# An attention and mixture-of-experts kernel: where memory rows are gated, when copies are issued, and which engine splits weights

## The chip, the cores and the metric

The kernel runs on one core of a Trainium2 chip. The metric is the device time of one execution in microseconds. The core has five instruction streams, each in program order: PE (TensorE, matrix products), ACT (ScalarE), DVE (VectorE), POOL (GpSimd) and SP, which here issues nearly all DMA transfers.

## The reference, cut to what matters

```
scores = (q @ k.T) / 8, causal;  local = softmax(scores) @ v
q_p = elu(q) + 1
mem = (q_p @ M_prev) / (q_p @ z_prev + 1e-6)
x = g * mem + (1 - g) * local          # g = sigmoid(beta), per head
h = relu(x @ w1[e]);  out += p[:, e] * (h @ w2[e])      # e = 0..3
```

There are 4 batches of 8 heads, 576 positions of 64 features each, so 2304 tokens of 512 features; four experts map 512 to 1024 to 512. All is float32 at the interface. The kernel gets its accuracy from split operands: a tensor is written as a high part (rounded) and a low part (the rest), and a product is three matmuls, high by high, high by low and low by high.

## The kernel before, in words

**Attention** is cut into runs (one batch and either its query blocks 0 and 1, called joint, or its blocks 2 to 4) and each run into four tasks, one for a pair of heads. The first run is written out by hand as a list of words (`ORDER`, in `first_run`). Tasks 0 to 27 are numbered over the other runs; tasks 0 to 11 are the joint ones. Each task is a set of steps, and each step stands in a list with a slot (its time on a planner's scale), a rank within the slot and a weight. The steps named below are `batch_load` (L234: loads z_prev broadcast to all partitions as `zb` and M_prev as `mr`, once per run; L239 multiplies `zb` by the gate on POOL), `t_phi1` to `t_phi4` (L300 to 343: elu, its product with `zb` in `rl`, its normaliser `rn`, the normalised `qp`), `t_trq` and `t_trk` (L381, L411: transpose q or k on PE and split it into `qa`, `qb` or `kha`, `khb`, `kl` by ACT and DVE) and `t_cpq` and `t_cpk` (L396, L420: DMA copies within the chip's memory, of q's high part to `qz` and of k's high parts to the other half of the partitions). The scores (`j_qk`, L474) read `qa`, `qz`, `kha`, `khb` and `kl`. `t_load` (L282) fetches q, k and v of a later task.

**Experts** run as phases. A phase is one half of one expert's hidden features for a group of 256 tokens or for two groups at once. Groups start at phases 0, 5, 8, 16 and 16 (`START`) and last 8 phases each, so that phases 0 to 4 and 13 to 15 hold a single group (`ALONE`) and the others two; after phase 23 (`PASS` is 24) eight more phases take the remaining tokens in another form. A phase has 16 parts of the first product (`mm1`, L862: four blocks `fc` of 128 hidden features, four parts each) and then the second product (`mm2`, L887: per tile of 128 tokens four parts, which read `w2s[0]` to `w2s[3]` in turn). After the last part of a block ACT writes the relu's high part `hh` (L880) and DVE its low part `hl` (L881).

**Weights** come by DMA into six buffers `stg`, a fixed order ahead (`w_dma`, L194). `w_prep` (L212) takes the next one: the high part by ACT (L225) or by POOL (L227), the low part always by POOL (L228), and then issues the next `w_dma` on SP, which waits until a buffer is free. A block of w1 for the next phase is prepared during the second product of the phase before; a block of w2 is prepared at the first part of the same block of the first product, by the call `after()` in `mm1`. In `first_run` the words w0 to w7 prepare w1 and w2 of phase 0, with high parts by POOL; between w1 and w2, between w3 and w4 and between w6 and w7 steps of the coming tasks are run, `batch_load` of task 0's run among them just ahead of w4.

**Interleaving**: a planner walks through the parts of the phases. Ahead of each part it runs steps while the weights done so far lie below a straight line against the estimated cost of the parts done. Before a group's first phase it runs all steps that the group's tokens need, and then `x_split` (L820) copies the group's tokens as a high part by ACT (L828) and a low part (L830) by DVE or POOL.

Of the kernel before, what the change touches and what calls it, by code (L numbers as in the profile page):

```python
# [11 lines left out]
ALU = mybir.AluOpType  # L12
# [37 lines left out]
def tile_attention_moe(  # L50
# [13 lines left out]
    nc = tc.nc  # L64
    P = 128
    B, H, S, D = q.shape
# [8 lines left out]
    CA, CB = (0, 1), (2, 3, 4)  # L75
# [23 lines left out]
    START = [0, 5, 8, 16, 16]  # L99
    PASS = START[-1] + NPH  # L100
# [13 lines left out]
    def ctile(shape, dt, name, pool=cst):  # L114
        return pool.tile(shape, dt, tag=name, name=name, bufs=1)

    def f(ap):
        return ap.bitcast(F32)
# [13 lines left out]
    gate = ctile([P, H], F32, "gate")  # L132
# [5 lines left out]
    for i in range(2):  # L138
# [49 lines left out]
    ALONE = [  # L188
        i for i in range(PASS) if sum(s_ <= i < s_ + NPH for s_ in START) == 1
    ]  # L190
# [3 lines left out]
    def w_dma():  # L194
        j = wpos["dma"]
        if j >= len(wseq):
            return
        wpos["dma"] += 1
        i, kind, fc = wseq[j]
        e, hf = halves[i]  # L200
        f0 = (hf * HF + fc) * P
        t = sp.tile([P, DM], F32, tag="stg", name=f"stg{j}", bufs=NSTG + 2)
        stg[j] = t
        if kind == "1":
            nc.sync.dma_start(
                out=t.rearrange("p (c f) -> p c f", c=NKD),
                in_=w1[e, :, f0 : f0 + P].rearrange("(c p) f -> p c f", p=P),
            )
        else:
            nc.sync.dma_start(out=t, in_=w2[e, f0 : f0 + P, :])  # L210

    def w_prep(i, kind, pool=False):  # L212
        act = (kind == "1" or i in ALONE or i >= PASS - 1) and not pool
        j = wpos["prep"]
        if j >= len(wseq) or wseq[j][0] != i or wseq[j][1] != kind:
            return
        wpos["prep"] += 1
        fc = wseq[j][2]
        t = stg.pop(j)
        hi, lo = (w1s if kind == "1" else w2s)[fc]  # L220
        if kind == "1":
            hi = hi.rearrange("p c f -> p (c f)")
            lo = lo.rearrange("p c f -> p (c f)")
        if act:
            nc.scalar.activation(hi, t, AF.Copy)  # L225
        else:
            nc.gpsimd.tensor_scalar(hi, t, 1.0, 1.0, ALU.mult, ALU.mult)  # L227
        nc.gpsimd.tensor_tensor(lo, t, f(hi), ALU.subtract)  # L228
        w_dma()


    bdat = {}

    def batch_load(r):  # L234
        b = r[0]
        zb = att.tile([P, H, D], F32, tag="zb", name=f"zb{b}_{r[1][0]}", bufs=2)
        nc.sync.dma_start(out=zb, in_=z_prev[b : b + 1].partition_broadcast(P)[:, 0])
        if b or r[1] == CB:
            nc.gpsimd.tensor_tensor(  # L239
                zb, zb, gate.unsqueeze(2).to_broadcast([P, H, D]), ALU.mult  # L240
            )
        mr = att.tile([P, H, D], F32, tag="mr", name=f"mr{b}_{r[1][0]}", bufs=1)
        for i in range(2):
            nc.sync.dma_start(
                out=mr[i * D : (i + 1) * D], in_=M_prev[b].rearrange("h d e -> d h e")
            )
        bdat[r] = [zb, mr, None]
# [16 lines left out]
    for b, cs in RUNS[1:]:  # L264
        for a in range(NPAIR):
            t = Task()
# [41 lines left out]
    def t_phi2(t):  # L308
        n = len(t.cs)
        t.qp = att.tile([P, 3, 2, D], F32, tag="qp", name=f"qp{t.i}", bufs=2)  # L310
        t.rl = att.tile([P, 3, 2, D + 1], F32, tag="rl", name=f"rl{t.i}", bufs=1)
        nc.vector.scalar_tensor_tensor(
            t.qp[:, 0:n], t.nat["q"][:, 0:n], 1.0, t.ex[:, 0:n], ALU.add, ALU.max
        )
        zb = bdat[t.run][0][:, 2 * t.a : 2 * t.a + 2].unsqueeze(1)
        nc.gpsimd.tensor_tensor(
            t.rl[:, 0:n, :, 0:D], t.qp[:, 0:n], zb.to_broadcast([P, n, 2, D]), ALU.mult
        )
        nc.gpsimd.tensor_scalar(
            t.rl[:, 0:n, :, D],  # L320
            gate[:, 2 * t.a : 2 * t.a + 2].unsqueeze(1).to_broadcast([P, n, 2]),
            1e-6,
            1.0,
            ALU.mult,
            ALU.mult,
        )
# [18 lines left out]
    def tr(dst, src, n):  # L345
        nc.tensor.transpose(dst, src, ident[0:n, 0:n])  # L346

    def to_tile(name):
        return ps.tile([P, 512], F32, tag="to", name=name, bufs=2)
# [28 lines left out]
    def flat(ap):  # L378
        return ap.rearrange("p j d -> p (j d)")

    def t_trq(t):  # L381
        pt = to_tile(f"tq{t.i}")
        qk, last = t.qk, t.nk == NCH
        w = len(t.cs) * P
        for i in range(len(t.cs)):

            tr(pt[:, i * P : (i + 1) * P], flat(t.nat["q"][:, i]), P)
        if last:
            tr(pt[:, w : w + P], flat(t.nat["k"][:, 4]), P)
        split_q(pt, qk["qa"], qk["qb"], w, SCALE)  # L390
        if last:
            split_k(pt[:, w:], qk, 4 * P, D)
        if t.i < 2:
            t_cpq(t)

    def t_cpq(t):  # L396
# [14 lines left out]
    def t_trk(t):  # L411
        pt = to_tile(f"tk{t.i}")
        m = min(t.nk, NCH - 1)
        for c in range(m):
            tr(pt[:, c * P : (c + 1) * P], flat(t.nat["k"][:, c]), P)
        split_k(pt, t.qk, 0, m * P)
        if t.i < 2:
            t_cpk(t)

    def t_cpk(t):  # L420
# [323 lines left out]
    for t in tasks:  # L744
        s0 = t.s0
        ld = -9 + t.i if t.i < 2 else s0 - 7
        PQ = PR
        n = len(t.cs)
        if t.run not in seen:
            seen.add(t.run)  # L750
            ev(s0 - (9 if t.i else 8), 9, lambda r=t.run: batch_load(r))
            ev(s0 + (2 if t.joint else 3), 9 if t.joint else 0.1, lambda r=t.run: batch_prep(r))
            if t.cs == CB and t.b == 0:
                for i in range(2):
                    ev(s0 - 12, 9, lambda i=i: zeros(i))
        ev(ld, 6.3 if t.cs == CA else 8, lambda t=t: t_load(t))
        ev(s0 + PQ["phi1"][0], PQ["phi1"][1], lambda t=t: t_phi1(t))
        ev(s0 + PQ["phi2"][0], PQ["phi2"][1], lambda t=t: t_phi2(t), 0.0, dv(n * P))
        ev(
            s0 + PQ["phi3"][0],  # L760
            PQ["phi3"][1],
            lambda t=t: t_phi3(t),
            0.0,
            600.0 if t.joint else 750.0,
        )
        ev(s0 - 3, 20, lambda t=t: t_phi4(t))
        ev(s0 + PQ["trq"][0], PQ["trq"][1], lambda t=t: t_trq(t), 109.0 * n, 2 * dv(n * P))
        ev(s0 + PQ["trk"][0], PQ["trk"][1], lambda t=t: t_trk(t), 109.0 * t.nk, 2 * dv(4 * P))
        if t.i >= 2:
            ev(s0 + PQ["trq"][0] + 1, 0.5, lambda t=t: t_cpq(t))  # L770
            ev(s0 + PQ["trk"][0], 2.4, lambda t=t: t_cpk(t))
        ev(s0, PQ["v"], lambda t=t: t_v(t))
        ev(
            s0 + PQ["trqp"][0 if t.joint else 2],
            PQ["trqp"][1],
            lambda t=t: t_trqp(t),
            109.0 * n,
            2 * dv(t.nq),
        )
    for i, s in slots.items():  # L780
        w = wid(s.c)
        t = s.t
# [37 lines left out]
    def x_split(n):  # L820
        for tt in range(2):
            o0 = (n % 2) * GW + tt * P
            o = slice(o0, o0 + P)
            r = rslot.pop((n, tt))
            rfree.append(r)
            rfree.sort()
            r = slice(r * P, (r + 1) * P)
            nc.scalar.activation(xh[:, :, o], xr[:, :, r], AF.Copy)  # L828
            sub = nc.gpsimd if n == 3 or (n == 4 and tt) else nc.vector
            sub.tensor_tensor(xl[:, :, o], xr[:, :, r], f(xh[:, :, o]), ALU.subtract)  # L830


# [29 lines left out]
    def mm1(i, fc, cols, after):  # L862
        wh, wl = w1s[fc]
        pt = []

        def part(c):
            if c == 0:
                pt.append(ps.tile([P, 512], F32, tag="moe", name=f"h{i}_{fc}", bufs=3))
                after()
            for z, (w_, x_) in enumerate(((wh, xh), (wh, xl), (wl, xh))):  # L870
                nc.tensor.matmul(  # L871
                    pt[0][:, cols],
                    lhsT=w_[:, c],
                    rhs=x_[:, c, cols],
                    start=(c == 0 and z == 0),
                    stop=(c == NKD - 1 and z == 2),
                )
            if c == NKD - 1:
                h_, l_ = hh[fc][:, cols], hl[fc][:, cols]
                nc.scalar.activation(h_, pt[0][:, cols], AF.Relu)  # L880
                nc.vector.scalar_tensor_tensor(  # L881
                    l_, pt[0][:, cols], 0.0, f(h_), ALU.max, ALU.subtract
                )

        return [lambda c=c: part(c) for c in range(NKD)]

# [721 lines left out]
```

## Time and profile before

| | us |
|---|---|
| runs of before: median (lowest, highest) | 1018.58 (1015.73, 1021.09) |
| the profiled execution | 1019.5 |
| its span, from the first to the last instruction | 1017.7 |
| PE busy in the span | 990.3 |
| ACT, DVE, POOL busy | 547.2, 650.4, 597.4 |
| mean granted clock of PE | 0.989 of full |

A busy PE is not a PE at its peak: its instructions overlap, and at half the clock the same product is busy for twice as long. So both the idle time of PE and the stretches of lowered clock are to be read.

### The profile page before, as it was taken

The page shows a single profiled execution, that of the slowest core. Times are in us where ns is not written, and L with a number is a line of the kernel's source. Part 1 is how long each engine was busy: PE and PEld are TensorE (multiplying, and loading weights), DVE is VectorE, ACT ScalarE, POOL GpSimd, SP SyncE. Part 2 cuts the span into 40 slices and gives each one's busy share as a digit, 9 for nine tenths or more (in the row PEclk, how much of TensorE's full clock was granted, in tenths as well). Part 3 has the DMA queues.
Part 4 walks back from the last instruction along what each step waited for, and adds up shares of the span by engine and source line. Part 5 has one row for each costly group of instructions (what it writes and reads, how often), then busy time and mean ns, then how long its engine had stood idle before and what let it go on. Part 6 is the DMA issues. An engine that isn't in the chain of part 4 may idle for free.

```text
span 1017.7 us, 16092 instructions
## 1 busy us (share of the span) xinstructions
PE 990.3 (97%) x5118; PEld 832.3 (82%) x5118; DVE 650.4 (64%) x1669; ACT 547.2 (54%) x1274; POOL 597.4 (59%) x614
## 2 busy tenths in 40 slices
PE   8798989999999999999999999999999999999998
PEld 6687878887888889888888888878888888888887
DVE  6477867887887878878777788664153342442533
ACT  7476745666666668866666665554243242342430
POOL 5578865775567547966564665394563554635630
PEclk9799989999999999999999999999999999999999
DMA  6566553544553446654453443222121121211102
GB/s 150 131 166 188 155 141 104 136 127 117 123 139 101 121 138 168 178 160 125 120 134 101 108 107 96 59 94 83 52 58 48 51 55 50 62 42 52 53 1 83
DMA packets 192149, 106.24 MB, mean 104 GB/s; under 512 B 99648, under 2 KB 170432, under 8 KB 192064
## 3 DMA queue, kind: packets, MB, share of 16 engines
q1 hardware_dynamic: 191760, 105.07, 38.6%
q8 instruction: 41, 0.67, 0.3%
q14 instruction: 44, 0.36, 0.1%
q10 hardware_dynamic: 304, 0.14, 0.1%
HBM read 90.09 MB, written 4.72 MB: 93 GB/s over the span
## 4 chain that ended last, share of the span: by engine, by line
PE 86%; POOL 4%; DMA 3%; DVE 2%; ACT 2%; issue 1%; SPq 1%; ACTq 0%; POOLq 0%; DVEq 0%
PE y L900 19%; PE h L871 18%; PE y L1172 17%; PE x L1096 9%; PE z L1096 4%; PE pt L346 4%; PE sp L612 4%; PE o L722 4%; PE y L1096 2%; POOL w2l L228 1%; PE tq L346 1%; PE sp L474 1%; PE tk L346 1%; PE o L560 1%; POOL w L228 1%
## 5 line engine op out<-in xcount | busy, mean ns | idle before, releaser
L228 POOL TENSOR_TENSOR w2l<-stg,w2h 128x512 fp32r<-128x512 f32 x128 | 167.7, 1314 | 146.2 <-ACT w2h L225 140.9
L871 PE MATMUL h<-xh,w 128*128 128x512 f32 (+1 forms) x768 | 248.5, 373 | 1.2 <-POOL w L228 1.2
L228 POOL TENSOR_TENSOR w<-stg,w 128x512 fp32r<-128x512 f32 x96 | 127.2, 1330 | 146.6 <-ACT w L225 135.6
L871 PEld LDWEIGHTS h<-xh,w 128*128 128x128 f32 x768 | 141.1, 192 | 18.8 <-POOL w L228 1.4
L900 PE MATMUL y<-w2h,hh 128*128 128x512 f32 x320 | 137.0, 428 | 2.0 <-POOL w2h L227 1.8
L871 PE MATMUL h<-xl,w 128*128 128x512 f32 (+1 forms) x384 | 137.6, 358 | 0.0
L900 PE MATMUL y<-w2l,hh 128*128 128x512 f32 x320 | 126.9, 397 | 3.0 <-POOL w2l L228 3.0
L900 PE MATMUL y<-w2h,hl 128*128 128x512 f32 x320 | 126.8, 396 | 0.0
L1189 DVE SCALAR_TENSOR_TENSOR acc<-y,pn,acc 128x512 f32<-128x512 f32 (+1 forms) x57 | 41.6, 740 | 82.2 <-PE y L1172 82.2
L661 ACT ACTIVATE pth<-pt 128x384 fp32r<-128x384 f32 (+3 forms) x128 | 50.2, 419 | 56.7 <-PE pt L346 55.5
L871 PEld LDWEIGHTS h<-xl,w 128*128 128x128 f32 x384 | 74.3, 193 | 5.9
L900 PEld LDWEIGHTS y<-w2h,hl 128*128 128x128 f32 x320 | 60.6, 189 | 13.7
L900 PEld LDWEIGHTS y<-w2l,hh 128*128 128x128 f32 x320 | 61.2, 191 | 12.1 <-POOL w2l L228 5.0
L900 PEld LDWEIGHTS y<-w2h,hh 128*128 128x128 f32 x320 | 60.9, 190 | 10.7 <-POOL w2h L227 2.2
L881 DVE SCALAR_TENSOR_TENSOR hl<-h,hh 128x512 fp32r<-128x512 f32 (+1 forms) x96 | 57.6, 600 | 17.8 <-ACT hh L880 16.5
L880 ACT ACTIVATE hh<-h 128x512 fp32r<-128x512 f32 (+1 forms) x96 | 50.4, 525 | 29.3 <-PE h L871 28.2
L346 PE MATMUL pt<-ident,s 128*128 128x128 f32 (+1 forms) x376 | 61.5, 274 | 1.5 <-DVE s L517 1.2
L346 PEld LDWEIGHTS pt<-ident,s 128*128 128x128 f32 (+1 forms) x376 | 47.1, 140 | 16.0 <-issue 1.6
L225 ACT ACTIVATE w<-stg 128x512 fp32r<-128x512 f32 x92 | 57.1, 625 | 0.7
L663 DVE TENSOR_TENSOR ptl<-pt,pth 128x384 fp32r<-128x384 f32 (+1 forms) x96 | 51.4, 549 | 9.3 <-ACT pth L661 8.0
L916 DVE SCALAR_TENSOR_TENSOR acc<-y,pn,acc 128x512 f32<-128x512 f32 x70 | 52.1, 745 | 7.4 <-PE y L900 6.9
L1120 DVE TENSOR_TENSOR cp_a<-y,cp_a 128x512 f32<-128x512 f32 x16 | 11.1, 692 | 71.4 <-PE y L1096 71.4
(272 smaller groups left out, 2562.6 us busy)
## 6 DMA issues: line engine op xcount, KB each, us to landing
stg<-in_moe_w_dram SPq DMA_DIRECT2D x256, 256.0 KB, 3.0
natall<-in_k_dram SPq DMA_DIRECT2D x34, 128.0 KB, 2.6
natall<-in_v_dram SPq DMA_DIRECT2D x32, 128.0 KB, 2.5
natall<-in_q_dram SPq DMA_DIRECT2D x60, 64.0 KB, 2.6
out_dram<-acc SPq DMA_DIRECT2D x15, 256.0 KB, 2.0
kha<-kha SPq DMA_DIRECT2D x16, 128.0 KB, 2.3
khb<-khb SPq DMA_DIRECT2D x16, 128.0 KB, 2.3
natall<-in_k_dram SPq DMA_DIRECT2D x28, 64.0 KB, 2.5
```

The costliest lines, as they stand in the source:

```text
L225: nc.scalar.activation(hi, t, AF.Copy)
L228: nc.gpsimd.tensor_tensor(lo, t, f(hi), ALU.subtract)
L346: nc.tensor.transpose(dst, src, ident[0:n, 0:n])
L661: nc.scalar.activation(dh, src, AF.Copy)
L663: nc.vector.tensor_tensor(dl, src, f(dh), ALU.subtract)
L871: nc.tensor.matmul(pt[0][:, cols], lhsT=w_[:, c], rhs=x_[:, c, cols], start=(c == 0 and z == 0), stop=(c == NKD - 1 and z == 2),)
L880: nc.scalar.activation(h_, pt[0][:, cols], AF.Relu)
L881: nc.vector.scalar_tensor_tensor(l_, pt[0][:, cols], 0.0, f(h_), ALU.max, ALU.subtract)
L900: nc.tensor.matmul(pt[0], lhsT=h_[fc][:, tk], rhs=w_, start=(fc == 0 and z == 0), stop=(fc == HF - 1 and z == 2),)
L916: nc.vector.scalar_tensor_tensor(acc[g, tt], pt[0], pe, acc[g, tt], ALU.mult, ALU.add)
L1096: nc.tensor.matmul(k_, lhsT=w_[:, c], rhs=x_[:, c], start=new and n == 0, stop=n == 5, skip_group_check=True,)
L1172: nc.tensor.matmul(y0, lhsT=a[:, tk], rhs=w_[:, x0:x1], start=(fc == 0 and z == 0), stop=(fc == HF - 1 and z == 2),)
```

## The change

It does four things. The product of `zb` with the gate moves from `batch_load` to `t_phi2` of the run's first task, right ahead of the first instruction that reads the product. The joint tasks from 2 on call `t_cpq` and `t_cpk` at the end of `t_trq` and `t_trk`, as tasks 0 and 1 did already, and not as steps of their own later on. In the phases with a single group `after()`, the preparation of a w2 block, stands behind the relu of the same block and not ahead of the block's first product; and in phases 5 to 7 too the high parts of w2 are written by ACT. For the groups that start at phases 5 and 8 the low part of the second tile goes from DVE to POOL; for the other groups it stays as it was.

```diff
 def w_prep(i, kind, pool=False):
-    act = (kind == "1" or i in ALONE or i >= PASS - 1) and not pool
+    act = (kind == "1" or i in ALONE or i < START[2] or i >= PASS - 1) and not pool
...
 def batch_load(r):
...
     nc.sync.dma_start(out=zb, in_=z_prev[b : b + 1].partition_broadcast(P)[:, 0])
-    if b or r[1] == CB:
-        nc.gpsimd.tensor_tensor(
-            zb, zb, gate.unsqueeze(2).to_broadcast([P, H, D]), ALU.mult
-        )
...
 def t_phi2(t):
...
-    zb = bdat[t.run][0][:, 2 * t.a : 2 * t.a + 2].unsqueeze(1)
+    zb = bdat[t.run][0]
+    if t.a == 0:
+        nc.gpsimd.tensor_tensor(
+            zb, zb, gate.unsqueeze(2).to_broadcast([P, H, D]), ALU.mult
+        )
+    zb = zb[:, 2 * t.a : 2 * t.a + 2].unsqueeze(1)
...
 def t_trq(t):
...
-    if t.i < 2:
+    if t.joint:
         t_cpq(t)
...
 def t_trk(t):
...
-    if t.i < 2:
+    if t.joint:
         t_cpk(t)
...
-    if t.i >= 2:
+    if not t.joint:
         ev(s0 + PQ["trq"][0] + 1, 0.5, lambda t=t: t_cpq(t))
         ev(s0 + PQ["trk"][0], 2.4, lambda t=t: t_cpk(t))
...
 def x_split(n):
...
-    sub = nc.gpsimd if n == 3 or (n == 4 and tt) else nc.vector
+    sub = nc.gpsimd if n == 3 or tt else nc.vector
...
 def mm1(i, fc, cols, after):
...
     if c == 0:
...
-        after()
+        if i not in ALONE:
+            after()
...
     if c == NKD - 1:
...
         nc.vector.scalar_tensor_tensor(
             l_, pt[0][:, cols], 0.0, f(h_), ALU.max, ALU.subtract
         )
+        if i in ALONE:
+            after()
```

## Rows read from the trace of the kernel before

**Rows 1.** The page, part 1: busy time of each engine.
```profile
PE 990.3 (97%) x5118; PEld 832.3 (82%) x5118; DVE 650.4 (64%) x1669; ACT 547.2 (54%) x1274; POOL 597.4 (59%) x614
```

**Rows 2.** Waits of PE, 30 to 160 us: waiter, releaser, total us, times, longest.
```profile
PE sp L474 <- DVE qa L356: 6.5, 1, 6.5
PE sp L474 <- DMA qz<-qa: 3.9, 3, 2.1
PE y L900 <- POOL w2h L227: 1.8, 1, 1.8
PE pt L346 <- DVE s L517: 1.2, 1, 1.2
PE h L871 <- POOL w L228: 1.2, 1, 1.2
PE y L900 <- POOL w2l L228: 1.2, 2, 0.9
PE sp L474 <- POOL qz L406: 0.8, 1, 0.8
```

**Rows 3.** Timeline of PE: start, us, instruction, idle before and releaser.
```profile
42.52 0.47 PE L474 MATMUL sp<-kha,qa 128*128 128x128 f32 x1 [6.46 <-DVE qa L356]
...
91.03 0.33 PE L474 MATMUL sp<-kl,qz 128*128 128x128 f32 x1 [2.11 <-DMA qz<-qa]
...
145.30 0.50 PE L900 MATMUL y<-w2h,hh 128*128 128x512 f32 x1 [1.75 <-POOL w2h L227]
...
235.00 0.66 PE L346 MATMUL tk<-ident,natall 128*128 128x128 f32 x4 [1.71 <-DMA natall<-in_k_dram]
```

**Rows 4.** Windows: stretch, length, busy PE PEld DVE ACT POOL (instructions), PEclk, DMA, GB/s.
```profile
40.00:50.30 10.30, 6.95 (x31) 6.76 (x32) 6.98 (x27) 1.71 (x7) 6.64 (x12) 0.51 0.28 69
...
91.00:94.50 3.50, 3.47 (x14) 3.18 (x15) 1.43 (x6) 1.37 (x5) 3.27 (x6) 0.54 0.72 231
146.00:152.70 6.70, 6.03 (x21) 5.45 (x22) 2.10 (x6) 1.39 (x3) 3.10 (x3) 0.50 0.53 142
```

**Rows 5.** Timeline of POOL, same columns as rows 3.
```profile
33.54 1.04 POOL L239 TENSOR_TENSOR zb<-zb,gate 128x512 f32<-128x512 f32 x1 [7.16 <-DMA zb<-in_z_prev_dram]
...
40.35 0.72 POOL L316 TENSOR_TENSOR rl<-qp,zb 128x256 f32<-128x256 f32 x1
...
43.36 0.41 POOL L406 TENSOR_SCALAR qz<-qa 64x256 fp32r<-64x256 f32 x1
...
77.29 1.04 POOL L239 TENSOR_TENSOR zb<-zb,gate 128x512 f32<-128x512 f32 x1 [3.24 <-DMA zb<-in_z_prev_dram]
...
142.44 1.04 POOL L239 TENSOR_TENSOR zb<-zb,gate 128x512 f32<-128x512 f32 x1 [3.46 <-DMA zb<-in_z_prev_dram]
```

**Rows 6.** Timeline of DVE, the normaliser of task 0.
```profile
41.38 0.42 DVE L332 TENSOR_REDUCE rn<-rl 128x4 f32<-128x260 f32 x1 [7.70 <-POOL rl L319]
```

**Rows 7.** Timeline of ACT: a copy it issues, a relu, a high part.
```profile
33.05 0.55 ACTq L373 DMA_DIRECT2D khb<-khb  x1
...
60.69 0.39 ACT L880 ACTIVATE hh<-h 128x256 fp32r<-128x256 f32 x1
...
61.44 0.63 ACT L225 ACTIVATE w2h<-stg 128x512 fp32r<-128x512 f32 x1
```

**Rows 8.** DMA issues, 20 to 170 us: engine, count, size, us to landing.
```profile
khb<-khb ACTq DMA_DIRECT2D x1, 64.0 KB, 4.7
```

**Rows 9.** Chain of waits, 62 to 125 us: start, us, what.
```profile
86.67 4.31 DMA qz<-qa
...
102.12 1.39 PE y L900 x6
```

**Rows 10.** Windows, phase 0's end to phase 4's end, columns as rows 4.
```profile
41.40:125.20 83.80, 76.19 (x480) 68.37 (x481) 64.72 (x213) 57.92 (x153) 65.45 (x69) 0.93 0.57 155
```

**Rows 11.** Line 830, both engines: ns least, median, most; first and last start.
```profile
L830 DVE TENSOR_TENSOR xl<-xr,xh x5: 680/1076/1776, 119.4 to 428.9; 128x512 fp32r<-128x512 f32 x5
...
L830 POOL TENSOR_TENSOR xl<-xr,xh x3: 1294/1296/1303, 395.3 to 428.1; 128x512 fp32r<-128x512 f32 x3
```
## The prediction

> **What bounds the kernel now.** I read the busy times first. PE is busy for 990.3 of 1017.7 us [rows 1]; the next busiest engine, DVE, has a third of the span free (PEld, the weight loads, runs beside PE). So a change pays only where PE stands idle or runs at a lower clock. The waits of PE come next: from 30 to 160 us they add up to 6.5 + 3.9 + 1.8 + 1.2 + 1.2 + 1.2 + 0.8 = 16.6 us [rows 2], and their releasers are what the change touches: task 0's `qa`, the `qz` copies, w2 and w1 from POOL, one DVE step. The timeline of PE gives their places [rows 3]. The windows then show what a long wait costs beyond itself: in three stretches the clock is half of full, 1.2 in place of 2.4 GHz [rows 4]. Each begins during or just after a wait over 2 us (at 145 us two waits with one product between them), and PE then works at half speed until the clock returns. The matmuls in them would have taken about half as long: 6.95 x 0.49 = 3.4 us, 3.47 x 0.46 = 1.6 us and 6.03 x 0.5 = 3.0 us, 8.0 us together. No such stretch follows the wait of 1.71 us at 235 us [rows 3]. So 24.6 us are in play.
>
> Last I asked POOL's timeline why the releasers were late: three times it stood at the gate product until z_prev landed, 7.16, 3.24 and 3.46 us, with weights queued behind [rows 5].
>
> **Task 0's z.** POOL's wait of 7.16 us begins at 33.54 - 7.16 = 26.38 us. Behind it stand three preparations of w2, which take from 34.58 to 40.35 us, 1.92 us each, and then `rl` [rows 5]; the normaliser `rn` waits for that on DVE for 7.70 us, with task 0's `qa` behind it [rows 6], and PE waits for `qa`. After the change the three preparations run from 26.4 to 32.2 us, inside the wait; their loads stand ahead of z's in SP's order. z's place among SP's transfers is the same, so it still lands at 33.5 us. The gate ends at 34.6 us and `rl` 1.0 us later, so `rn` starts at 35.6 us and not 41.38 us, 5.8 us earlier. The fourth preparation and the two `qz` halves follow: POOL begins them at 37.5 us where it was 43.36 us [rows 5]. One input does not move: `khb`'s copy is issued by ACT at 33.05 us [rows 7] and takes 4.7 us to land [rows 8], so 37.8 us, just not later. PE therefore passes its second wait at about 37.9 us and not 43.8 us. Of 6.5 + 0.8 us some 1.6 us stay, in two pieces, each below the wait that left the clock alone [rows 3]; I take it that the clock holds, which gives the 3.4 us as well. If it falls all the same, the nearest row is the short stretch, 1.6 us [rows 4]. Gain 7.3 - 1.6 + 3.4 = 9.1 us, bounds 7.5 and 10.7 us.
>
> **The later z's.** At 77.29 us the gate holds up POOL for 3.24 + 1.04 us, and behind it come the last block of w1 and all of w2 of phase 2. PE's waits for `w` (1.2 us) and part of those for `w2l` (1.2 us in two) follow from it. At 142.44 us it holds up the last w2 of phase 5 for 3.46 + 1.04 us; PE waits 1.75 us for `w2h` [rows 3] and the rest of the `w2l` sum [rows 2]. At the new places z has landed three slots before. The product itself (1.04 us) is moved, not saved; it sits then behind less urgent work. In phases 5 to 7 POOL also loses its twelve high parts; ACT takes them at 0.63 us each [rows 7], 7.6 us over three phases, with time to spare [rows 1]. Gain 1.2 + 1.2 + 1.8 us, and the 3.0 us of clock that follow the wait at 145 us: 7.2 us.
>
> **Copies at once.** Three times the scores wait for `qz`, 3.9 us in all [rows 2]; the worst, 2.11 us [rows 3], is a copy issued at 86.67 us that took 4.31 us [rows 9]. The copy now follows the transposes by which it is fed, a slot earlier; 2.1 us earlier is enough for all three. What it adds is a wait on SP: the copy blocks SP until ACT has split q or k, and behind it stand loads of weights and of later tasks. Those weights are asked for four preparations ahead, some 5 us of POOL's time at 1.3 us for a low part, against landings like the 4.31 us here; so I take nothing for it, and keep as upper bound that the 3.9 us come back as load waits. Gain 3.9 + 1.6 us of clock. Ten tasks also lose two steps of weight 100 each, by the code 2,000 of 555,890: steps run about one part earlier for a while. I take zero, within 1.5 us either way.
>
> **Tokens' low part.** The two of phase 4 hold up DVE, and PE waits 1.2 us for `s` on DVE [rows 2]. One now goes to POOL. DVE takes 680 to 1776 ns for it, POOL 1296 [rows 11]: one less frees at least 0.7 us there, probably over 1.6 us, since these are the slow ones. I take the whole 1.2 us. POOL pays 1.3 us.
>
> The Trainium skill ("GPSIMD Engine Reference", section 4.1, Engine selection) speaks against this part: two-input elementwise work belongs on VectorE, GpSimd being about half as fast. The best rows agree with it (1296 against 680 ns), and by them DVE would gain 0.7 us, not 1.2, for POOL's 1.3; the sum below would be 19.1 us.
>
> **w2 behind the relu.** In single-group phases the last block's preparation starts after its relu. The chain from the end of the first product is relu 0.39, high part 0.63 [rows 7], low part 1.30 (the same shape as in rows 11): 2.3 us. PE comes to this block's low part after nine matmuls of 0.23 us [rows 9] and one more, 2.3 us, plus whatever attention lies between. So it is even if ACT and POOL are free, with no cover to spare. No row shows it queued. Bounds: nothing, or one POOL item of 1.3 us in each of the seven phases (1 to 4, 13 to 15), 9.1 us. I take 0.3 us each, 2.1 us, near the lower end since attention work mostly lies between.
>
> **POOL nearer its limit.** From 41.4 to 125.2 us POOL is busy 65.45 of 83.8 us [rows 10]. The waits that go there (0.8 + 3.0 of the `qz` sum + 1.2 + 0.3 + 1.2 + 1.1 of task 0's) and 5.0 us of clock shorten the stretch to some 71 us, while the low part makes POOL's work 66.8 us: 94%. I charge one item, 1.3 us.
>
> **Sum**: 9.1 + 7.2 + 5.5 + 1.2 - 2.1 - 1.3 = 19.6 us, from the profiled execution's 1019.5 us (span 1017.7 and 1.8 around it): **1000 us**. That execution stands 0.9 us above the median.
>
> **Rivals.**
> 1. POOL becomes late in the single-group phases: at 94% in-order work, one more low part stands before each last w2. For it: the even chain above, and POOL's extra work. Against: the z product no longer blocks it. Time: 1019.5 - 23.0 (all gains) + 9.1 + 1.3 = 1007 us. The page of the Trainium skill named above ("GPSIMD Engine Reference", section 4.1) is on this rival's side.
> 2. What comes before phase 5 is mostly given back: with PE ahead, and SP blocked by the early copies, the loads become the wait. For it: DMA is 57% busy over that stretch already [rows 10]. Against: PE shows hardly any wait for a load there [rows 2]. What is left is phase 5's share (1.8 + 0.9 + 3.0) less 2.1: 1016 us.
> 3. Slower: in each single-group phase POOL gets to w2 only when the first product is over, a whole set of four low parts, 4 x 1.3 = 5.2 us, against some 2.5 us of cover: 2.7 us, past the length after which the clock fell, so 1.6 us more. Seven times 4.3 is 30 us: 1019.5 - 23.0 + 30 = 1026 us. It decides from 3.3 us per phase on. Against: the first three blocks are prepared during the product.
> 4. That the change does not do what it says: the gate at its new place could stand waiting too. For task 0 it does, from 32.2 to 33.5 us, counted above; for later runs z has long landed. No case of its own.
>
> **Chances.** Forecast 0.63; rival 1 0.25; rival 2 0.08; rival 3 0.04. A measurement here can tell about 0.5%, 5 us. Faster by more than that is the first two, 0.88; within it 0.08; slower 0.04. The range goes from 994 us (every gain, no charge, and 2.5 us for the spread of single runs and the reordering) to 1009 us (rival 1 with the clock falling once).
>
> **What would show it.** The changed profile should have no wait of POOL for z longer than 2 us, `rn` of task 0 at about 35.6 us, PE at the scores by 37 us, no lowered clock between 37 and 160 us, no wait for `qz`, phase 5 begun some 17 us earlier, and PE waits for `w2l` of a few tenths in phases 1 to 4 and 13 to 15. Waits of over 1 us there, or for `stg` loads on ACT, would make it wrong; so would `rn` still behind 40 us.

## The result, and the profile after

Six executions of the changed kernel took 1003.65 us in the median (1002.73 to 1006.57), six of the kernel before, run beside it, 1018.98 us (1015.73 to 1021.09): a ratio of 0.9859 [0.9836, 0.9882], so 1.4% faster. The profiled execution took 1003.48 us, its span is 1001.4 us.

Part 1 of the page, after (compare [rows 1]):

```profile
PE 982.7 (98%) x5118; PEld 823.8 (82%) x5118; DVE 650.8 (65%) x1667; ACT 551.2 (55%) x1286; POOL 595.5 (59%) x604
```

PE does the same 5118 matmuls in 7.6 us less busy time: 6.2 us less from phase 0 to phase 16, where it no longer works at half clock anywhere, and 1.5 us less before phase 0 (last section). The timeline of POOL at task 0 (columns as [rows 5]):

```profile
32.28 1.05 POOL L313 TENSOR_TENSOR zb<-zb,gate 128x512 f32<-128x512 f32 x1 [1.14 <-DMA zb<-in_z_prev_dram]
33.40 0.74 POOL L317 TENSOR_TENSOR rl<-qp,zb 128x256 f32<-128x256 f32 x1
...
36.42 0.40 POOL L407 TENSOR_SCALAR qz<-qa 64x256 fp32r<-64x256 f32 x1
```

and of DVE, the normaliser ([rows 6] before):

```profile
34.44 0.42 DVE L333 TENSOR_REDUCE rn<-rl 128x4 f32<-128x260 f32 x1 [2.51 <-POOL rl L320]
```

POOL's wait of 7.16 us for z is now 1.14 us, and `rn` starts at 34.44 us where it was 41.38. The other four waits for z, two of them in the first 160 us, are gone. What PE still waits for, over the whole span:

```profile
PE y L904 <- POOL w2l L228: 4.0, 7, 1.1
PE tk L347 <- DMA natall<-in_k_dram: 2.5, 2, 1.5
...
PE sp L475 <- DVE qa L357: 1.3, 1, 1.3
PE sp L475 <- POOL qz L407: 1.0, 1, 1.0
...
PE tp L347 <- POOL qp L339: 0.6, 1, 0.6
PE sp L475 <- DMA qz<-qb: 0.4, 1, 0.4
```

Task 0's 6.5 us are 1.3 us, the 3.9 us for copied `qz` are 0.4 us [rows 2]. The first line is now that of the low part of w2: 4.0 us in seven waits, where the kernel before has 3.0 us in five. Two of them, 1.4 us, lie in phase 23 in both kernels; in phases 13 to 15 it is 2.0 us where it was 0.4.

The windows below show three stages, cut at the first `h` product of a phase in PE's timeline: phases 0 to 5 (where the predicted gains lay), 6 to 12, and 13 to 16. Before, then after (columns as [rows 4]):

```profile
32.73:162.08 129.35, 112.74 (x664) 98.15 (x664) 91.33 (x298) 78.53 (x210) 94.31 (x105) 0.92 0.55 148
162.08:384.17 222.09, 220.36 (x1185) 186.04 (x1183) 179.96 (x515) 139.77 (x344) 138.32 (x150) 1.00 0.48 124
384.17:466.85 82.68, 81.94 (x508) 72.63 (x507) 66.35 (x179) 61.30 (x144) 65.16 (x58) 1.00 0.60 162
```

```profile
30.98:140.53 109.55, 104.90 (x665) 91.36 (x665) 89.24 (x301) 79.92 (x215) 88.36 (x98) 1.00 0.66 177
140.53:363.43 222.90, 220.57 (x1184) 185.92 (x1183) 177.96 (x510) 143.27 (x351) 134.88 (x142) 1.00 0.47 122
363.43:450.43 87.00, 83.36 (x509) 72.36 (x507) 69.22 (x180) 60.71 (x144) 64.68 (x57) 1.00 0.60 157
```

The first stage is 19.8 us shorter, the second 0.8 us longer, the third 4.3 us longer: 14.7 us. From phase 17 on the two kernels agree. The span is 16.3 us shorter; the rest, 1.75 us, lies before phase 0 and is not the change's (last section). So the gain came where it was forecast, and in this execution a quarter of it was given back in phases 6 to 16, for which the prediction had charged 0.9 us.

### The profile page after: what moved, and what is told of

Same layout as the page of the kernel before. It is cut to its first block, busy times and chain, and to the rows that moved or that the text cites. A ratio compares the mean times of both kernels' runs of the same rounds, so it can differ in the third digit from the quotient of the medians.

```text
span 1001.4 us, 16120 instructions
## 1 busy us (share of the span) xinstructions
PE 982.7 (98%) x5118; PEld 823.8 (82%) x5118; DVE 650.8 (65%) x1667; ACT 551.2 (55%) x1286; POOL 595.5 (59%) x604
## 4 chain that ended last, share of the span: by engine, by line
PE 79%; POOL 8%; issue 5%; DMA 3%; ACT 2%; SPq 2%; DVE 2%; POOLq 0%; ACTq 0%; DVEq 0%
PE y L1176 17%; PE y L904 16%; PE h L873 14%; PE x L1100 9%; PE z L1100 4%; PE sp L613 3%; PE pt L347 3%; PE o L723 3%; POOL w2l L228 3%; POOL w L228 2%; PE y L1100 2%; DMA stg<-in_moe_w_dram 1%; DMA natall<-in_k_dram 1%; PE tk L347 1%; PE tq L347 1%
## 5 line engine op out<-in xcount | busy, mean ns | idle before, releaser
L873 PE MATMUL h<-xh,w 128*128 128x512 f32 (+1 forms) x768 | 244.8, 370 | 0.0
L873 PEld LDWEIGHTS h<-xh,w 128*128 128x128 f32 x768 | 138.6, 189 | 17.9 <-POOL w L228 0.3
L637 ACT ACTIVATE s<-s,st 128x384 f32<-128x384 f32 (+2 forms) x80 | 54.7, 684 | 0.3
```

The lines of the kernel that those rows point to most:

```text
L637: nc.scalar.activation(s.s[:, 0:w], s.s[:, 0:w], AF.Exp, bias=s.st[:, 0:1], scale=-1.0, accum_out=s.st[:, 2:3],)
L873: nc.tensor.matmul(pt[0][:, cols], lhsT=w_[:, c], rhs=x_[:, c, cols], start=(c == 0 and z == 0), stop=(c == NKD - 1 and z == 2),)
```

## Experiments

Twelve kernels. Beside each ratio to the kernel before (of the same runs) stand the lengths of the three stages in its profiled execution, one execution each. Small differences in these columns show little by themselves: in phases 13 to 16 the kernels e7 and e10 are the changed kernel, instruction by instruction, and yet take 85.26 and 86.29 us against its 87.00, and one fall of the clock adds 1.6 us or more to a stage.

| kernel | median us | ratio [95%] | phases 0-5 | 6-12 | 13-16 |
|---|---|---|---|---|---|
| before | | 1 | 129.35 | 222.09 | 82.68 |
| the change | 1003.65 | 0.9859 [0.9836, 0.9882] | 109.55 | 222.90 | 87.00 |
| e1 z alone | 998.68 | 0.9817 [0.9794, 0.9840] | 109.62 | 222.34 | 81.45 |
| e2 all but z | 1014.77 | 0.9971 [0.9956, 0.9986] | 122.03 | 222.03 | 86.49 |
| e3 copies alone | 1013.38 | 0.9961 [0.9946, 0.9976] | 119.47 | 223.10 | 85.51 |
| e4 all but copies | 999.59 | 0.9819 [0.9800, 0.9838] | 109.46 | 221.17 | 85.14 |
| e5 all, w2 ahead again | 999.46 | 0.9821 [0.9797, 0.9845] | 109.31 | 222.72 | 84.16 |
| e6 all, weight kept | 1000.23 | 0.9824 [0.9801, 0.9848] | 107.63 | 222.39 | 85.29 |
| e7 all, high parts on POOL | 1005.12 | 0.9871 [0.9848, 0.9894] | 111.20 | 224.92 | 85.26 |
| e8 z, low part | 999.33 | 0.9806 [0.9780, 0.9833] | 108.94 | 223.74 | 81.45 |
| e9 z, low part, copies with weight | 997.67 | 0.9807 [0.9791, 0.9824] | 109.82 | 222.34 | 82.25 |
| e10 all but the low part | 1008.30 | 0.9904 [0.9888, 0.9921] | 110.55 | 224.18 | 86.29 |
| e11 z, copies with weight | 998.25 | 0.9806 [0.9790, 0.9822] | 110.20 | 222.28 | 82.32 |
| e12 all, weight kept, w2 behind early only | 999.98 | 0.9824 [0.9807, 0.9840] | 108.72 | 221.95 | 83.89 |

**e1, z alone.** The kernel before with one part of the change:

```diff
 def batch_load(r):
-    if b or r[1] == CB:
-        nc.gpsimd.tensor_tensor(zb, zb, gate..., ALU.mult)
 def t_phi2(t):
+    if t.a == 0:
+        nc.gpsimd.tensor_tensor(zb, zb, gate..., ALU.mult)
```

> The kernel before with the gate product of z moved and nothing else. Theory A (POOL's stand at the z product is the root of most waits, those for the qz copies too, since SP stood behind POOL): phase 0 gains 7.9 us as in the changed kernel, phases 1 to 2 some 4 us, phase 5 some 4 us, in all 14 to 16 us, about 1003 to 1005 us. Rival B (each part of the change takes away waits of its own): only task 0's 9 us and the waits of PE for w and w2l, 3 us of them, go; the 3.9 us for qz and their clock stay: about 1008 us.

0.9817: better than the whole change (the two intervals touch), and more than theory A's 14 to 16 us. Its stages:

```profile
31.32:140.94 109.62, 104.25 (x665) 91.49 (x665) 90.48 (x298) 78.03 (x210) 89.37 (x100) 1.00 0.67 176
140.94:363.28 222.34, 220.59 (x1185) 185.94 (x1184) 179.90 (x515) 140.06 (x344) 138.85 (x150) 1.00 0.47 123
363.28:444.73 81.45, 81.45 (x509) 72.67 (x507) 65.50 (x179) 61.24 (x144) 65.51 (x58) 1.00 0.62 164
```

Up to phase 6 the z part earns 19.7 us by itself, as much as all four parts do (19.8), and in phases 13 to 16 PE is never idle: 81.45 of 81.45 us. The waits from 30 to 141 us, against [rows 2]:

```profile
PE pt L347 <- DVE s L518: 1.8, 2, 1.1
PE sp L475 <- DVE psm L855: 1.6, 1, 1.6
PE sp L475 <- DMA qz<-qa: 0.7, 1, 0.7
PE sp L475 <- DMA qz<-qb: 0.5, 1, 0.5
PE sp L475 <- DMA khb<-khb: 0.5, 1, 0.5
```

The copies are steps of their own as before, yet the 3.9 us of waits for `qz` are 1.2 us: with z moved most of them go. The queue of SP shows the way. In the kernel before, from 76 to 82 us, SP has one wait:

```profile
SPq L205 <- POOL w L228: 4.6, 1, 4.6
```

POOL came to that block of w1 only after the gate product of 77.29 us [rows 5], and behind the load of weights that SP then issued, at 80.78 us, stand the loads of q, k and v and the copy of 86.67 us [rows 9]. In e1 the same wait of SP, from 64 to 69 us, is 0.3 us.

**e2, all but z.** The changed kernel with that hunk undone.

> The changed kernel with the gate product back at the load. Theory A: nearly everything is lost, 1015 us or more, with a wait of over 6 us at the first scores and a lowered clock after it. Rival B: the copies, w2 and the low part still take away 5.5 + 1.2 us and some of phase 5: about 1010 us.

0.9971, nearly what theory A has (1014.8 against 1015 us or more). The first stage takes 122.03 us. POOL stands at z again at task 0; PE's timeline there, and in phase 5 a wait of 3.0 us for `w2l`, show what it costs:

```profile
41.37 0.47 PE L474 MATMUL sp<-kha,qa 128*128 128x128 f32 x1 [6.92 <-DVE qa L356]
42.66 0.47 PE L474 MATMUL sp<-kl,qz 128*128 128x128 f32 x1 [0.82 <-POOL qz L406]
```

So z's part is worth 12.5 us of the first stage inside the whole change and 19.7 us alone. The others are worth 7.3 us there while POOL still stands at z (129.35 against 122.03), and 0.1 us once z is moved.

**e3, copies alone.** The kernel before with:

```diff
 def t_trq(t):      # the same in t_trk, with t_cpk
-    if t.i < 2:
+    if t.joint:
         t_cpq(t)
...
-    if t.i >= 2:
+    if not t.joint:
         ev(...t_cpq(t)); ev(...t_cpk(t))
```

> The kernel before with the joint tasks' copies issued at once and nothing else. Rival B: the three waits for qz (3.9 us) and 1.6 us of clock go: about 1013 us. Theory A: the copies still stand behind POOL on SP in the worst case (2.1 us and the clock), so 1 to 3 us: 1016 to 1018 us.

0.9961, 3.9 us, between the two expectations. Theory A was wrong on the waits: those for a copied `qz` are all gone though SP still stands behind POOL, 5.3 us here: the copies are asked for early enough to bear it. So either part takes these waits away, and they can be earned once. The first stage is 9.9 us shorter, and in phase 5, where PE waits 0.34 and 0.87 us for w2 and not 1.75 and 0.87, the clock holds. But the wait for w1's weights in phase 2 (`PE h <- POOL w`) grows from 1.2 to 2.1 us, and the stages behind lose 1.0 and 2.8 us: in phase 16 PE waits 1.0 us for `qp` of POOL. This kernel prepares w2 as before; the copies alone disturb phases 13 to 16.

**e4, all but the copies.** The changed kernel with the hunk of e3 undone.

> The changed kernel with the copies back as steps of their own. Rival B: 4 to 5.5 us are lost: 1008 to 1009 us, with waits for qz of over 2 us in all. Theory A: at most 2 us are lost, under 1006 us; and if the reordering of the steps by the copies' lost weight costs the 3 to 4 us that came back between phases 13 and 17, it is even faster than the changed kernel, by up to 3 us.

0.9819, 4 us faster than the change, as theory A with the reordering has it. The first stage is as short without the copies (109.46 us). In phase 16 no wait is left. Phases 13 and 14 still wait for `w2l`, four times:

```profile
PE y L904 <- POOL w2l L228: 2.3, 4, 0.9
```

**e5, w2 ahead again.** The changed kernel with the fourth hunk undone:

```diff
 def mm1(i, fc, cols, after):
     if c == 0:
-        if i not in ALONE:
-            after()
+        after()
     if c == NKD - 1:
-        if i in ALONE:
-            after()
```

> The changed kernel with w2's preparation ahead of the first product again in the single-group phases; the rest of the change stays. Theory C (w2 behind the relu costs more than it gives, in phases 13 to 15 above all, where the changed kernel waits 0.7 + 1.1 + 0.2 us for w2l and the z-alone kernel not at all): 3 us faster than the changed kernel, about 1000.5 us, with no wait for w2l between 360 and 415 us. Rival D (the waits there come from the steps' new order): the same time as the changed kernel, 1003 to 1004 us.

0.9821. The waits for `w2l` in phases 2 and 3 are gone, 0.28 and 0.27 us, and these phases are 0.56 and 0.51 us shorter (phase 1, where a wait for DVE goes, 0.62 us); phase 13 is 0.95, phase 15 0.53 and phase 16 1.26 us shorter. The kernels that have the change's order and its w2 (e2, e7, e10) take 17.1 us for phase 13 as the change does, but 33.4 to 33.7 us for phase 16 where it takes 34.1, so that 0.6 to 0.9 of the 1.26 us are left beyond that spread. In phase 14 a wait of 0.9 us for DVE takes the place of that for `w2l`. In this execution the clock fell once in phase 0, which costs 1.6 us of the first stage.

**e6, weight kept.** The changed kernel; the two steps that the joint tasks no longer have leave their weight of 100 each with the transposes, so that the planner's line stands where it was:

```diff
+cw = 100.0 if t.joint and t.i >= 2 else 0.0
-ev(..., t_trq(t), 109.0 * n, 2 * dv(n * P))
+ev(..., t_trq(t), 109.0 * n, 2 * dv(n * P) + cw)     # t_trk alike
```

> The changed kernel, but the weight of the copies' former steps is put on the transposes that now issue them, so that the planner's line is as before. Theory E (the waits in phase 16, 0.6 us for qp and 1.1 us for k, and part of phase 8's, come from the shifted order): they go, 2 to 3 us faster than the changed kernel, 1001 us. Rival F (they come from the copies' own place on SP): they stay, 1003 to 1004 us.

0.9824, as theory E has it (1000.2 us), and in the profiled executions 4.1 us less from phase 0 to phase 17: 1.9 in the first stage, 0.5 in the second, 1.7 in the third. Every copy is issued by the same step as in the change; only the order of the steps against the products differs. Phase 16, which has 1.62 us of idle in the change (0.9 to 1.2 in e2, e7 and e10), has none here; phases 13 and 14 still wait 2.35 us for `w2l`, as in e4. That the third stage of e7 is as short (85.26 us) without this edit says that the 1.7 us there are not all the order's.

```profile
32.57:140.20 107.63, 104.50 (x664) 91.40 (x663) 89.07 (x297) 79.86 (x214) 87.51 (x97) 1.00 0.66 177
...
362.59:447.88 85.29, 82.93 (x509) 72.28 (x507) 69.79 (x179) 60.84 (x144) 65.14 (x58) 1.00 0.59 157
```

**e7, high parts on POOL.** The changed kernel with `i < START[2]` taken out of `w_prep`'s condition again.

> The changed kernel with the high parts of w2 in phases 5 to 7 back on POOL. If ACT's taking them is what clears phase 5, that phase becomes 2 to 4 us longer, 1006 to 1008 us. If the moved z product alone clears it (the z-alone kernel has phase 5 shorter by 1.3 us than the changed one), nothing changes or it is 1 us faster: 1002.5 to 1004 us.

0.9871, the same as the change within the intervals. Phase 5, where the high parts were, took 31.53 us against 31.62. The longer first and second stages are two falls of the clock, in phases 0 and 8. The third stage, 1.7 us shorter, has the same instructions as in the change: its waits for `w2l` in phase 14 and for k in phase 16 are 0.39 and 0.38 us and not 1.12 and 1.05. Which engine makes these high parts does not matter here.

**e8, z and the low part.** e1 and `n == 3 or tt` in `x_split`.

> The kernel before with the z product moved and the tokens' low part shared, nothing else. Against z alone (998.7 us) the wait of 1.1 us for DVE's s at the end of phase 4 should go: 997.5 us; if POOL's extra subtraction makes w late there, as the rule on GpSimd has it, 998.5 to 1000 us.

0.9806: not told apart from e1. Phase 4 is 1.71 us shorter, as the wait of 1.08 us for DVE goes, but phase 5 is 0.85 us longer, with new waits for `qz` (0.47 us) and `ptl` (0.25 us), phase 1 is 0.80 us longer, with a wait of 1.14 us where z alone has 0.74, and in phase 8 the clock fell after a wait of 1.87 us. The time is that of the second expectation, but by these waits and not by a late `w`.

**The last four** ask whether the parts add up once the order is kept and w2 is ready early (theory K in what follows), or whether z is the one part that pays (theory L). e9 is e8 with the copies as in e6, e11 is e1 with the copies as in e6. e10 is the change with `x_split` as before. e12 is e6 with this in `mm1`:

```diff
-if i not in ALONE:
+if i >= START[1]:      # ahead of the product from phase 5 on
     after()
...
-if i in ALONE:
+if i < START[1]:       # behind the relu in phases 0 to 4 alone
     after()
```

> The kernel before with three of the parts: the z product at its first use, the tokens' low part shared, and the joint tasks' copies issued at once with their steps' weight put on the transposes; w2 stays ahead of the first product and its high parts on POOL. Theory K (the parts add up where the order is kept and w2 is ready early): the gain of z alone (18 us) plus the qz waits of up to 0.7 us, phase 4's 1.7 us and about 1 us in phase 8, so a ratio of 0.977 to 0.980, no wait for w2l over 0.3 us in phases 13 to 15, and a span of 992 to 995 us. Theory L (z is the one part that pays; what the others save in one phase they pay back in the next, as the low part did): 0.981 to 0.983, with new waits of 0.5 us or more for s, qz or h's weights in phases 1, 5 or 8.

> The kernel before with the z product moved and the joint tasks' copies issued at once, their weight kept on the transposes; low part and w2 as before. Theory K: z alone plus the qz waits, 0.7 us, and 0.5 to 1 us in phase 8: a ratio of 0.979 to 0.981. Theory L: 0.981 to 0.983. By either no tp or tk wait over 0.5 us in phase 16.

0.9807 and 0.9806, on the border of the two expectations. Both intervals overlap that of z alone, so no further gain is shown. The two kernels differ by the low part alone, and that adds nothing here. e9's stages:

```profile
32.38:142.20 109.82, 105.53 (x664) 93.23 (x664) 89.01 (x297) 77.84 (x210) 90.07 (x100) 0.98 0.67 176
142.20:364.54 222.34, 220.54 (x1184) 185.95 (x1183) 180.49 (x514) 140.16 (x344) 140.77 (x152) 1.00 0.47 124
364.54:446.79 82.25, 82.14 (x508) 72.41 (x507) 66.25 (x179) 61.31 (x144) 65.58 (x58) 1.00 0.60 162
```

With the order kept and w2 ahead, the copies at once cost only 0.8 us in phases 13 to 16 where the change lost 5.6 us against e1. In the first stage they save phases 1 and 2 some 0.9 us each, which the clock's fall in phase 0 and longer phases 3 and 5 take back.

> The changed kernel with the tokens' low part by VectorE again where it was. Theory K: phase 4 gets 1.2 to 1.7 us longer, by a wait for VectorE, and the ratio is 0.987 to 0.988. Theory L: what phase 4 loses comes back in phases 5 to 8, and the ratio stays at 0.985 to 0.987.

0.9904, further off than either theory said. The low part's share is larger inside the change: without it phase 4 is 0.84 us longer, phase 5 0.25 and phase 7 1.57 us, and phase 16 0.67 us shorter. The waits in phase 7 (two in PE's timeline, for `pth` of ACT and `ptl` of DVE, 0.39 and 0.34 us) come after the low parts of the next group, which the same hunk moves; that they come from them was not traced. That is 1.6 us net after phase 0's start, where the medians differ by 4.6 us; the profiled executions differ by 3.2 us in span, 1.7 of them before phase 0. Four of this kernel's five executions have a mean clock of 0.998, as have three of six of the change, so falls of the clock may be part of the rest; those executions left no trace, and the rest stays open.

> The changed kernel with the weight kept on the transposes, and w2 behind the relu in phases 1 to 4 alone; in phases 13 to 15 it is ahead of the first product again. Theory K: phases 13 and 14 take 16.2 and 15.9 us instead of 17.9 and 17.6, so 3 to 3.5 us less than the kernel with only the weight kept: a ratio of 0.978 to 0.981 and no w2l wait over 0.3 us from phase 5 on. Theory L: waits for h's weights or the copies take the place of w2l's in phases 13 to 16, and the ratio is 0.981 to 0.983.

0.9824, as theory L has it. Phase 13 does take 16.16 us again, but phase 14 takes 18.30 us: a wait of 1.30 us for `w2l` stays there, though w2 is asked for ahead of the product. In e9, with the same instructions there, phase 14 takes 15.87 us and has no such wait. So w2 behind the relu is not the one cause of that wait.

## Why the prediction was right, and where it was not

The forecast of 1000 us, its range, and "faster" held. Of the signs that it named, phase 5 begins 16.4 us earlier where 17 were forecast (1.75 us of it from the start), and no stretch of lowered clock is left between 37 and 160 us; of waits for a copied `qz` one of 0.4 us stays. By the steps:

**Task 0's z, right.** `rn` at 35.6 us was predicted, 34.44 us measured; PE past its second wait at 37.9, measured 36.87, both some 1.1 us sooner, after a start that was 1.75 us sooner. The two waits left are 1.29 and 0.97 us, 2.3 against 1.6 us, and the second is for `qz` of POOL, not for `khb`. In the profiled execution the clock held.

**The later z's, right in kind, too small.** Their waits, and the clock with them, are gone. But the prediction gave z 16.3 us (9.1 + 7.2), and alone it earns 19.7 us up to phase 6: 8.0 in phase 0 and 11.7, not 7.2, in phases 1 to 5.

**Copies at once, the step that failed.** I took the three `qz` waits for the copies' own: 3.9 us and 1.6 us of clock. e1 leaves the copies alone and has 1.2 of the 3.9 us, and no fall of the clock in phase 2, which is 4.26 us shorter. So the copy at 86.67 us [rows 9] was late because SP stood 4.6 us behind POOL, which had stood at z until 77.29 us [rows 5]. To issue the copies earlier is a second cure for the same waits (e3), worth 9.9 us of the first stage while z is where it was, and hardly anything after it: e4, without the copies, has the same first stage as the change, and in e9 and e11 phases 1 and 2 are 1.8 us shorter than in e1, which other phases take back. The 5.5 us were counted and not earned; z earned 3.4 us more than its terms. That the sum for the first stage (23.0, less the 1.2 of w2 in phases 1 to 4 and the 1.3 for POOL: 20.5 us) came out near the 19.8 us measured is these two errors against each other, and in so far luck.

**Reordering "zero, within 1.5 us", the other failure.** The lost weight of 2,000 in 555,890 moves steps ahead of the products. With the weight kept (e6) the profiled execution is 4.1 us shorter from phase 0 to phase 17; by the ratios of the medians it is 3.6 us (0.9859 and 0.9824, whose intervals just overlap), and e4, which has the old order too, says the same. So some 3.5 us, known to within about 3, stand against a charge of nothing. In phase 16 the chain of waits shows a place where it bites: six copies on SP, then loads, then the load of k for which PE waits 1.05 us at 431.37 us.

```profile
422.16 0.59 SPq L405
...
422.80 0.59 SPq L410
...
425.34 0.51 SPq L283
...
427.32 0.96 SPq L283
```

That the copies stand in SP's queue is not enough, since e6 issues the same copies and does not wait. Nor does the order alone fix the length: in e2, e7 and e10, with the change's order, the same wait is 0.60, 0.38 and 0.32 us. That is as far as the runs go: they don't say which step's shift decides.

**w2 behind the relu, mis-sized.** 2.1 us were charged. The waits are 2.57 us (0.28 + 0.27 in phases 2 and 3, 0.68 + 1.12 + 0.22 in phases 13 to 15; the rest of the line above lies in phase 23, in e1 too). Taking w2 ahead again gives 3.3 us of phases 1 to 3 and 13 to 15, more than the waits themselves, and at least 0.6 us more in phase 16. One sign by which the prediction was to be wrong came true: a wait of over 1 us in these phases, the 1.12 us of phase 14. The timelines of ACT and POOL show how it arose. Phase 14 begins at 380.58 us; ACT first, then POOL:

```profile
385.80 0.22 ACT L367 ACTIVATE kha<-tq 64x64 fp32r<-64x64 f32 x1 [2.19 <-DVE qb L360]
...
386.28 0.38 ACT L882 ACTIVATE hh<-h 128x256 fp32r<-128x256 f32 x1
386.56 0.62 ACT L225 ACTIVATE w2h<-stg 128x512 fp32r<-128x512 f32 x1
```

```profile
387.26 1.31 POOL L228 TENSOR_TENSOR w2l<-stg,w2h 128x512 fp32r<-128x512 f32 x1 [3.42 <-DMA stg<-in_moe_w_dram]
389.35 1.30 POOL L228 TENSOR_TENSOR w2l<-stg,w2h 128x512 fp32r<-128x512 f32 x1 [0.78 <-ACT w2h L225]
390.60 0.84 POOL L339 TENSOR_TENSOR qp<-qp,rn 128x384 f32<-128x384 f32 x1
391.39 2.74 POOL L228 TENSOR_TENSOR w2l<-stg,w2h 128x512 fp32r<-128x512 f32 x2
```

It is the chain of relu, high part and low part that I worked out, but without its condition that ACT and POOL be free. The relu of the first block stands in ACT's order behind an attention copy, before which ACT waited 2.19 us for DVE; high part and low part follow it, and the third block, for which PE waits until 392.91 us, then queues on POOL behind an attention product. (The weights' load by which the profile ends POOL's first wait can't be that of this block: it landed at 387.2 us, and ACT read the block's own buffer from 386.56 us on.) The bound of one queued item per phase was in the text, but phases 13 to 15 took it and phases 1 to 4 hardly did.

The two causes do not visibly add up: either one undone alone brings the ratio to about 0.982 (e5, e6), both together to 0.981 (e9, where the high parts also stay on POOL), and the intervals, 0.002 either way, could hide a part of a sum.

**POOL near its limit, not reached.** The stretch from the first scores to phase 5 was predicted to shrink to some 71 us with POOL at 94%. After, from the first scores at 35.59 us:

```profile
35.60:108.90 73.30, 71.39 (x481) 63.94 (x481) 61.18 (x209) 56.99 (x153) 63.94 (x68) 1.00 0.67 180
```

It is 73.3 us, with 0.97 us of wait for task 0's `qz` and 0.55 us for `w2l` in it, and POOL is busy for 63.94 of them, 87%. Behind task 0, PE waits for POOL there by no more than these 0.55 us, which are w2's. So the charge of 1.3 us for a further late item, and rival 1 as worked out for phases 1 to 4, are not borne out; what rival 1 describes happened in phases 13 and 14.

**Low part, open.** 1.2 us were taken. Beside z alone it takes away the wait in phase 4 and pays it back (e8), and between e11 and e9 it earns nothing; inside the change it is worth 4.6 us by the medians (e10), most of which is not accounted for. I had seen one instruction move; the hunk moves two, in phase 4 and in phase 7. The rule of the Trainium skill ("GPSIMD Engine Reference", section 4.1, Engine selection) agrees with the durations after as well, 1.30 us on POOL against 0.72 us on DVE in the median for the same tile, and yet the move is no loss in any of these pairs: the wait that it takes away in phase 4 is one for DVE.

**Rival 2** (given back as load waits) had its mechanism in phase 16, for a direct wait of 1.05 us, not for 16. **Rival 3** did not occur: the longest `w2l` wait in question is 1.12 us, against the 3.3 us per phase from which it decides.

The profiled execution misses the forecast by 3.5 us, the median by 3.7. The 3.5 us are 4.2 us given back in phases 6 to 16 beyond the charge (14.7 - 19.8 = -5.1, against -0.9), 0.7 us by which the first stage is short of its forecast, and 0.4 us behind phase 17 and outside the span, with 1.75 us the other way from the start. A version that beats both kernels exists: e9 (z, low part, copies with the weight kept), with an interval that ends at 0.9824, below the change's; e11 does the same with less. Moving z alone is nearly all of it.

## What to carry to other kernels

When one engine stands in order at a late input, waits that follow on other engines, more than 10 us later, may be its own; price the other parts of a change as if that wait were already gone, or they are counted twice. In a kernel whose order is planned by costs, a change of the costs is a change of the order: keep the planned weight when a step is merged into another, and test that by itself. And preparing an operand "just in time" where the engines are even is no saving, since it leaves no cover when one of the engines in its chain is held up.

## What the runs showed of the hardware

**The clock after short waits.** Two waits at task 0, 1.46 and 0.96 us in e9, 1.48 and 0.98 us in e4, have different ends. PE's timeline in e9, then in e4:

```profile
37.17 0.33 PE L475 MATMUL sp<-kha,qa 128*128 128x128 f32 x1 [1.46 <-DVE qa L357]
38.47 0.33 PE L475 MATMUL sp<-kl,qz 128*128 128x128 f32 x1 [0.96 <-POOL qz L407]
```

```profile
35.86 0.33 PE L475 MATMUL sp<-kha,qa 128*128 128x128 f32 x1 [1.48 <-DVE qa L357]
37.16 0.33 PE L475 MATMUL sp<-kl,qz 128*128 128x128 f32 x1 [0.98 <-POOL qz L407]
```

Windows that begin about 1.8 us after the second wait, in e9 and then in e4:

```profile
40.30:43.70 3.40, 3.40 (x18) 3.40 (x18) 2.77 (x15) 1.46 (x6) 1.38 (x4) 0.50 0.19 42
```

```profile
39.00:42.40 3.40, 3.40 (x27) 3.22 (x27) 2.77 (x15) 2.57 (x9) 1.38 (x4) 1.00 0.20 45
```

At half clock PE did 18 instructions in this stretch, at full clock 27. In the changed kernel the waits are 1.29 and 0.97 us and the clock held; in e5 they are 1.34 and 0.97 us and it fell; in e1 they are 1.62 and 0.53 us and it held. The length of the waits alone does not decide, and a fall costs some 1.6 us, a third of what these runs can tell apart.

**The start.** PE's matmuls come to their full speed about 4.5 us sooner in some executions than in others. The same eight matmuls, before and after:

```profile
5.84 1.66 PE L1269 MATMUL pf<-tw,tw 64*128 64x128 f32 x8 [0.61 <-DVE tw L1258]
```

```profile
5.75 0.93 PE L1273 MATMUL pf<-tw,tw 64*128 64x128 f32 x8 [0.61 <-DVE tw L1262]
```

From 6 to 10 us, before and then after:

```profile
6.00:10.00 4.00, 4.00 (x18) 2.79 (x20) 2.52 (x15) 2.90 (x12) 0.00 (x0) 1.00 0.91 192
```

```profile
6.00:10.00 4.00, 3.86 (x30) 2.67 (x29) 2.91 (x18) 3.26 (x13) 0.00 (x0) 1.00 0.87 192
```

The rows give a granted clock of 1.00 for both, so that this is the clock is not shown; the durations are all there is. Phase 0 began at 30.7 to 31.3 us in eight of the fourteen profiled executions, in which the eight matmuls took 0.93 us, and at 32.4 to 32.7 us in the other six, in which they took 1.65 or 1.66 us, with and without each part of the change. Two single profiles can differ by 1.7 us for this alone.
